# Receptance units on halves of the array's rows, spread between score chunks, in an attention and channel-mix kernel

## Chip, core and metric

The kernel runs on one core of one Trainium2 chip. The metric is the device time of one execution in microseconds, the median of several runs.

## What is computed

Sigmoid attention over 8 batches, 12 heads, 448 positions and 64 columns per head, and then an RWKV-like channel mix on its output x (8 x 448 x 768). Weights come as 64-bit floats.

```python
scores = q @ k.T / sqrt(64) - log(448)
x = sigmoid(scores) @ v                 # heads side by side: 768 columns
x_prev = x shifted by one position in each batch
xk = mu_k * x + (1 - mu_k) * x_prev
xr = mu_r * x + (1 - mu_r) * x_prev
kk = maximum(xk @ w_k, 0)               # 768 -> 1024
v = kk * kk @ w_v                       # 1024 -> 768
r = sigmoid(xr @ w_r)                   # 768 -> 768, the receptance
out = r * v
```

## The kernel before

Heads are taken in pairs: "head n" in the code and here is a pair of heads laid on the two halves of the 128 partitions, 48 of them, six to a batch. Positions 0 to 383 of the keys are three chunks of 128 (NC = 3), the last 64 are the tails.

`prepare` (L304) splits k and q of a head into a high part of type fp32r (ScalarE cast, L308) and the rest, the low part (VectorE subtraction, L309). `scores` (L332) multiplies one chunk of keys with all queries: three products (high-high, low-high, high-low), each as two matmuls, one for each half of the rows (64 partitions), into the two banks of a score tile `sc[u]`. `sigmoid` (L349) reads both banks with one ScalarE instruction of 896 columns into a tile `pf`. `weigh` (L362) multiplies a chunk of `pf` with v, the two heads on the two halves of the array's columns. The tails of two heads go through `score_tails` and `weigh_tails` on quarters of the array. `gather` (L379) takes the attention output of a head out of the bank, stores it to memory, forms xr and splits that too; for heads under R_FROM = 10 most of it is on ScalarE, from there on more is on VectorE.

There are three tiles `sc`, of two banks each. `turn` (L328) hands them out round: each user waits until the one three turns before it has been read.

A receptance unit (`receptance`, L398) is one block of 128 output columns of r for one batch: six blocks of xr, three matmuls for each (L406 to L408), on all 128 rows, 18 in all, into one bank; a sigmoid on ScalarE (L412) and a store of r follow. There are 48 units. 40 are placed in the attention, two in each loop from n=8 on; the last eight follow it, in a plan of their own.

The main loop (L470) takes two heads at a time, n = 0, 2, ..., 46. In it TensorE's order is: three chunks of scores of head n+1; then two receptance units (n >= 8) or the weighing of head n (n < 8); three chunks of scores of head n+2; weighings that are left; tails of the weighing (L374); tail scores of heads n+2 and n+3 (`last_keys`, L345). A light loop is here one without a receptance unit, a heavy loop one with.

Every step is handed to `Plan` with an engine, an estimated cost, a priority (about the number of the head at which it is due, small first) and what it reads and writes. `Plan.order` simulates the engines with these costs and writes out a fixed order for each engine; all engines then run their list in order. TensorE's steps depend on each other in a chain, so its order is that of the program text. SWITCH (L209) is an estimate of 190 ns that the plan adds to a step at which the use of the array's rows and columns changes.

`convert_wr` (L248) turns w_r from 64-bit floats into fp32r parts (five VectorE steps, a ScalarE cast, a VectorE subtraction), twelve pieces, with due times WR_PACE apart. `convert_seven` (L259) does the same for w_k and w_v, and stores sums that the second half needs; its due times begin after R_FROM (L447). After the attention the channel mix runs with seven products per block (L633), in a plan that has nothing of the change.

Of the kernel before, what the change touches and what calls it, by code (L numbers as in the profile page):

```python
# [10 lines left out]
AF = mybir.ActivationFunctionType  # L11
# [11 lines left out]
class Plan:  # L23
# [8 lines left out]
    def op(self, engine, cost, prio, run, reads, writes, dma=None):  # L32
        i = len(self.ops)
        deps = set()
        for r in reads:
            if r in self.writer:
                deps.add(self.writer[r])
        for w in writes:
            if w in self.writer:
                deps.add(self.writer[w])  # L40
            deps.update(self.readers.get(w, ()))
        for r in reads:
            self.readers.setdefault(r, []).append(i)
        for w in writes:
            self.writer[w] = i
            self.readers[w] = []
        deps.discard(i)
        self.ops.append(Op(engine, cost, prio, run, deps, dma))
# [50 lines left out]
def attention_then_channel_mix(  # L99
# [14 lines left out]
    nc = tc.nc  # L114
    P = 128
    N, _, S = q.shape
# [6 lines left out]
    NJ = DM // P  # L123
    NF = DF // P
    NC = S // P
# [25 lines left out]


    WP, PFB, PTB, LEAD, RAW = 512, 9, 2, 2, 4
    WR_PACE, W_PACE = 0.85, 0.9
    R_FROM = 10
    LATE = 2


# [52 lines left out]
    def mm(n, cols=S):  # L211
        return n * (cols * 0.447 + 3)

    def act(n, sbuf=False, ptr=False):
        return 51 + 0.834 * n + 42 * sbuf + 93 * ptr

    def dve(n, fast=False, ptr=False):
        return 69 + n / (1.92 if fast else 0.96) + 61 * ptr

    def dma(dst, src, prio, reads, writes):  # L220
        ns = dst.shape[0] * math.prod(dst.shape[1:]) * 4 / 300
        op(SP, 500, prio, lambda: nc.sync.dma_start(dst, src), reads, writes, dma=ns)
# [81 lines left out]
    def prepare(n, at):  # L304
        i = n % LEAD
        for src, hi, lo, a, w in ((kn[n % RAW][:, :KW], kh, kl, "k", KW), (qn[n % RAW], qh, ql, "q", S)):
            R = [(a + "n", n % RAW)]
            op(ACT, act(w, True), at, lambda src=src, hi=hi: nc.scalar.copy(hi[i], src), R, [(a + "h", i)])  # L308
            op(DVE, dve(w), at, lambda src=src, hi=hi, lo=lo: nc.vector.tensor_sub(lo[i], src, hi[i]), R + [(a + "h", i)], [(a + "l", i)])  # L309

    half = [slice(h * D, (h + 1) * D) for h in range(2)]
# [1 line left out]
    def pe(cost, go, reads, writes, at):  # L313

        op(PE, cost, at, go, reads, writes + ["order"])
# [5 lines left out]
    def qk(n):  # L321
        i = n % LEAD
        return [(a, i) for a in ("kh", "kl", "qh", "ql")]
# [4 lines left out]
    def turn():  # L328
        turns[0] += 1
        return (turns[0] - 1) % 3  # L330

    def scores(n, c, u, at):  # L332
        def go():
            for e, (kk, qq) in enumerate(products(n)):
                for h in range(2):
                    nc.tensor.matmul(sc[u][:, h, :S], kk[half[h], c * P:(c + 1) * P], qq[half[h], :], start=e == 0, stop=e == 2)  # L336

        pe(mm(3) + SWITCH * (c == 0), go, qk(n), [("sc", u, 0), ("sc", u, 1)], at)


    def score_tails(n, u, at):
# [7 lines left out]
    def sigmoid(n, c, u, at):  # L349
        if c < NC:  # L350
            i = (n * NC + c) % PFB
            f, K = pf[i], ("pf", i)
        else:
            i = n // 2 % PTB
            f, K = pt[i], ("pt", i)
        R = [("sc", u, 0), ("sc", u, 1)]
        op(ACT, act(2 * S), at, lambda: nc.scalar.activation(f, sc[u][:, :, :S], AF.Sigmoid, bias=NEG_LOG_S, scale=SCALE), R, [K])  # L357


    def weigh(n, c, at):  # L360
        i = (n * NC + c) % PFB

        def go():
            for h in range(2):
                nc.tensor.matmul(av[n % 2][half[h], :S], vn[n % 5][:, h * NC + c, :], pf[i][:, h, :], start=c == 0, stop=False)  # L365

        pe(752 + SWITCH * (c == 0) * (n % 2 == 0 or n < 8), go, [("pf", i), ("vn", n % 5)], [("av", n % 2)], at)


    def weigh_tails(n, at):  # L370
# [8 lines left out]
    def gather(n, at):  # L379
        b, j = divmod(n, NP)  # L380
        x, y = xx[n % 2], t1[n % 2]
        X, T = ("xx", n % 2), ("t1", n % 2)
        if n < R_FROM:
            op(ACT, act(S), at, lambda: nc.scalar.copy(x[:, 1:], av[n % 2][:, :S]), [("av", n % 2)], [X])  # L384
        else:
            op(DVE, dve(S), at, lambda: nc.vector.tensor_copy(x[:, 1:], av[n % 2][:, :S]), [("av", n % 2)], [X])  # L386
        dma(x_d[j][b], x[:, 1:], at, [X], [("x_d", n)])
        if n < R_FROM:
            op(ACT, act(S, True, True), at, lambda: nc.scalar.mul(y, x[:, :S], omr[:, j:j + 1]), [X, ("om", 0)], [T])  # L389
        else:  # L390
            op(DVE, dve(S, True, True), at, lambda: nc.vector.tensor_scalar(y, x[:, :S], omr[:, j:j + 1], None, ALU.mult), [X, ("om", 0)], [T])
        op(DVE, dve(S, ptr=True), at, lambda: nc.vector.scalar_tensor_tensor(y, x[:, 1:], mur[:, j:j + 1], y, ALU.mult, ALU.add), [X, T], [T])
        t, key = xr[j][:, :, b % 2 * S:(b % 2 + 1) * S], ("xr", j, b % 2)
        op(ACT, act(S, True), at, lambda: nc.scalar.copy(t[:, 0], y), [T], [key + ("hi",)])
        op(DVE, dve(S), at, lambda: nc.vector.tensor_sub(t[:, 1], y, t[:, 0]), [T, key + ("hi",)], [key + ("lo",)])

    def receptance(b, i, at, bank):
        t, tk = bank  # L398
# [44 lines left out]
    for nh in range(2):  # L443
        for j in range(NJ):
            convert_wr(j, nh, jt)
            jt += WR_PACE
    jt = max(R_FROM, jt)  # L447
    for w, out7, half_rows, n in ((w_k, wk_o, NJH, DF // 2), (w_v, wv_o, NFH, HN)):
        for t in range(half_rows):
            convert_seven(w, out7, t, half_rows, n, W_PACE, jt + 0.4)  # L450
# [1 line left out]
    units = [(b, i) for b in range(B - 1) for i in range(NJ)]  # L452
    late = units[len(units) - LATE:]
    units = units[:len(units) - LATE]
    def key_chunks(n, at):
        if n + 1 < N:
            prepare(n + 1, at + 0.6 - 5 * (n < R_FROM))
        us = [turn() for _ in range(NC)]
        for c in range(NC):
            scores(n, c, us[c], at)  # L460
            sigmoid(n, c, us[c], at + 0.1 * c)

    def last_keys(n, at):
        u = turn()
# [3 lines left out]
    key_chunks(0, 0)  # L468
    last_keys(0, 0)
    for n in range(0, N, 2):  # L470
        at = n + 1
        key_chunks(n + 1, at)
        if n + 3 < N:
            load(n + 3, at + 0.2 - 5 * (n < 4))
        if n >= 8:
            for _ in range(2):
                u = turn()
                if units:
                    receptance(*units.pop(0), at + 0.4, (sc[u][:, 0], ("sc", u, 0)))
        else:  # L480
            for c in range(NC):
                weigh(n, c, at)
        at = n + 2
        if n + 2 < N:
            key_chunks(n + 2, at)
        for i in range(n < 8, 2):
            for c in range(NC):
                weigh(n + i, c, at)
        weigh_tails(n, at)
        if n + 2 < N:  # L490
            last_keys(n + 2, at)
        if n + 4 < N:
            load(n + 4, at + 0.2 - 5 * (n < 4))
        gather(n, at + 0.45)
        gather(n + 1, at + 0.5)
# [246 lines left out]
```

## Time and profile before

| | |
|---|---|
| median of 3 runs | 854.35 us (852.76 to 854.6) |
| the profiled execution | 852.26 us |
| its span, first to last instruction | 850.5 us |
| TensorE busy | 834.7 us (98%) |
| VectorE busy | 600.5 us (71%) |
| ScalarE busy | 447.6 us (53%) |
| granted TensorE clock | 1.0 of full |
| attention, with its receptance units | about 0 to 412 us |
| last units and passage to the channel mix | about 412 to 450 us |
| channel mix | about 450 to 850 us |

A busy TensorE is one with a matmul in it; matmuls overlap, so a start-to-start time says what one costs, and its listed duration does not. ScalarE and VectorE instructions overlap their neighbours a little as well. An idle time in a row stands in square brackets behind it, with what ended it. PEld is the loading of weights into the array.

### The profile page before, as it was taken

How to read it: one execution, taken by the hardware profiler on the slowest of the kernel's cores; microseconds unless marked ns; L12 is line 12 of the kernel's file. 1: busy time of each engine (PE TensorE's matmuls, PEld its weight loads, DVE VectorE, ACT ScalarE, POOL GpSimd, SP SyncE). 2: the span in 40 equal slices, each digit the busy share in tenths (PEclk: the TensorE clock that was granted, in tenths of full speed). 3: DMA queues.
4: the chain of work that ended last, by engine and by line, in shares of the span. 5: the costliest groups of instructions: out<-in, count | busy, mean ns of one | idle time of the engine just before them, and what ended most of it. 6: DMA issues, size and time to landing. Idle time of an engine off the chain costs nothing.

```text
span 850.5 us, 13233 instructions
## 1 busy us (share of the span) xinstructions
PE 834.7 (98%) x4704; PEld 667.2 (78%) x4704; DVE 600.5 (71%) x1115; ACT 447.6 (53%) x758; POOL 0.5 (0%) x8
## 2 busy tenths in 40 slices
PE   7999999999999999999999999999999999999998
PEld 3456666776667776677789999999999999999997
DVE  5999888988334333342379987969789795886955
ACT  7995555655546555464378394563746333333330
POOL 0000000000000000000000000000000000000000
PEclk9999999999999999999999999999999999999999
DMA  8878898888334433341487553343654667473415
GB/s 256 257 242 285 295 310 281 285 288 281 122 111 154 151 118 118 109 141 44 153 286 246 166 183 101 138 140 120 217 181 147 204 184 239 135 238 121 141 60 163
DMA packets 90930, 157.65 MB, mean 185 GB/s; under 512 B 10352, under 2 KB 79472, under 8 KB 90864
## 3 DMA queue, kind: packets, MB, share of 16 engines
q1 hardware_dynamic: 90864, 156.81, 56.4%
q8 instruction: 37, 0.61, 0.3%
q14 instruction: 29, 0.24, 0.1%
HBM read 98.05 MB, written 58.72 MB: 184 GB/s over the span
## 4 chain that ended last, share of the span: by engine, by line
PE 90%; ACT 4%; DMA 3%; issue 1%; DVE 1%; SPq 0%; POOLq 0%; POOL 0%; DVEq 0%; ACTq 0%
PE xb L633 26%; PE yb L633 20%; PE av L365 12%; PE sc L336 10%; PE sc L406 6%; PE sc L407 6%; PE sc L408 6%; DMA x<-x_d 2%; PE av L374 2%; PE sc L345 2%; ACT pf L357 1%; ACT t L389 1%; DMA qn<-in_q 1%; ACT qh L308 0%; ACT xx L384 0%
## 5 line engine op out<-in xcount | busy, mean ns | idle before, releaser
L557 ACT CAST rr<-ys 128x448 fp32r<-128x448 f32 x135 | 73.8, 567 | 106.7 <-PE xb L633 41.6
L357 ACT ACTIVATE pf<-sc 128x896 f32<-128x896 f32 x144 | 125.5, 926 | 5.1 <-PE sc L336 5.1
L365 PE MATMUL av<-pf,vn 128*64 128x448 f32 x576 | 114.4, 544 | 0.0
L406 PE MATMUL sc<-xr,slot 128*128 128x448 f32 x288 | 106.6, 370 | 2.1 <-ACT pf L357 2.1
L407 PE MATMUL sc<-xr,slot 128*128 128x448 f32 x288 | 104.3, 362 | 0.0
L408 PE MATMUL sc<-xr,slot 128*128 128x448 f32 x288 | 104.2, 362 | 0.0
L633 PE MATMUL xb<-rr,slotc 128*128 128x448 f32 x450 | 93.0, 362 | 0.4 <-ACT p1s L662 0.4
L633 PE MATMUL yb<-rr,slot 128*128 128x448 f32 x450 | 92.9, 362 | 0.0
L558 DVE TENSOR_TENSOR rr<-ys,rr 128x448 fp32r<-128x448 f32 x135 | 80.4, 618 | 16.0 <-ACT rr L557 15.9
L309 DVE TENSOR_TENSOR kl<-kn,kh 128x384 fp32r<-128x384 f32 x48 | 26.7, 556 | 88.9 <-ACT kh L308 88.8
L633 PEld LDWEIGHTS xb<-rr,slotc 128*128 128x128 f32 x450 | 84.3, 187 | 6.4 <-ACT p1s L662 0.8
L633 PEld LDWEIGHTS yb<-rr,slot 128*128 128x128 f32 x450 | 84.4, 187 | 5.6
L365 PEld LDWEIGHTS av<-pf,vn 128*64 128x64 f32 x576 | 38.9, 136 | 62.4 <-issue 61.3
L336 PE MATMUL sc<-qh,kh 64*128 64x448 f32 x288 | 59.3, 408 | 7.0 <-ACT qh L308 4.5
L412 ACT ACTIVATE ro<-sc 128x448 f32<-128x448 f32 x48 | 26.1, 545 | 74.1 <-PE sc L408 61.7
L406 PEld LDWEIGHTS sc<-xr,slot 128*128 128x128 f32 x288 | 54.0, 188 | 12.6 <-ACT pf L357 8.3
L357 ACT ACTIVATE pt<-sc 128x896 f32<-128x896 f32 x24 | 22.2, 925 | 75.4 <-PE sc L345 75.4
L386 DVE COPY xx<-av 128x448 f32<-128x448 f32 x38 | 22.0, 621 | 50.4 <-PE av L374 50.4
L408 PEld LDWEIGHTS sc<-xr,slot 128*128 128x128 f32 x288 | 54.0, 187 | 3.7
L336 PEld LDWEIGHTS sc<-qh,kh 64*128 64x128 f32 x288 | 27.3, 186 | 37.5 <-issue 19.1
L407 PEld LDWEIGHTS sc<-xr,slot 128*128 128x128 f32 x288 | 54.1, 188 | 3.1
L336 PE MATMUL sc<-ql,kh 64*128 64x448 f32 x288 | 53.3, 366 | 0.0
(86 smaller groups left out, 1374.6 us busy)
## 6 DMA issues: line engine op xcount, KB each, us to landing
k_d<-cc SPq DMA_DIRECT2D x64, 224.0 KB, 2.0
kn<-in_k SPq DMA_DIRECT2D x48, 224.0 KB, 4.5
qn<-in_q SPq DMA_DIRECT2D x48, 224.0 KB, 4.7
vn<-in_v SPq DMA_DIRECT2D x48, 224.0 KB, 3.4
x_d<-xx SPq DMA_DIRECT2D x48, 224.0 KB, 3.8
r_d<-ro SPq DMA_DIRECT2D x48, 224.0 KB, 2.7
x<-x_d SPq DMA_DIRECT2D x48, 224.0 KB, 2.7
rt<-r_d SPq DMA_DIRECT2D x48, 224.0 KB, 2.9
```

The lines of the kernel that those rows point to most:

```text
L309: op(DVE, dve(w), at, lambda src=src, hi=hi, lo=lo: nc.vector.tensor_sub(lo[i], src, hi[i]), R + [(a + "h", i)], [(a + "l", i)])
L336: nc.tensor.matmul(sc[u][:, h, :S], kk[half[h], c * P:(c + 1) * P], qq[half[h], :], start=e == 0, stop=e == 2)
L357: op(ACT, act(2 * S), at, lambda: nc.scalar.activation(f, sc[u][:, :, :S], AF.Sigmoid, bias=NEG_LOG_S, scale=SCALE), R, [K])
L365: nc.tensor.matmul(av[n % 2][half[h], :S], vn[n % 5][:, h * NC + c, :], pf[i][:, h, :], start=c == 0, stop=False)
L386: op(DVE, dve(S), at, lambda: nc.vector.tensor_copy(x[:, 1:], av[n % 2][:, :S]), [("av", n % 2)], [X])
L406: nc.tensor.matmul(t[:, :S], wr_hi[j][:, rows], hi, start=(j == 0), stop=False)
L407: nc.tensor.matmul(t[:, :S], wr_lo[j][:, rows], hi, start=False, stop=False)
L408: nc.tensor.matmul(t[:, :S], wr_hi[j][:, rows], lo, start=False, stop=(j == NJ - 1))
L412: op(ACT, act(S), at, lambda: nc.scalar.activation(ro[u], t[:, :S], AF.Sigmoid), [tk], [("ro", u)])
L557: op(ACT, act(S, True), at, lambda: nc.scalar.copy(r[:, 0], y), [Y], [R])
L558: op(DVE, dve(S), at, lambda: nc.vector.tensor_sub(r[:, 1], y, r[:, 0]), [Y, R], [R + ("lo",)])
L633: nc.tensor.matmul(bank[:, :S], a, b, start=first and t == 0 and e == 0, stop=t == n - 1 and e == 2, skip_group_check=True)
```

## The change

It has four parts.

- A unit becomes `receptance_halves`: every matmul of it is cut into two, one for each half of the 128 rows, as the scores are. The halves' sums go into the two banks of one tile `sc[u]`. ScalarE copies one bank to `ro`, VectorE adds the other, ScalarE takes the sigmoid in place. The eight units after the attention keep the old form.
- Units stand apart from each other: in a heavy loop one after the third score chunk of head n+1 and one after the first score chunk of head n+2.
- Loops with units begin at n=10 instead of n=8; loops 10 and 12 have three units (the third after the second chunk of head n+2). Loop 8 weighs head n between the score chunks, as loops 0 to 6 do. The 40 units stay 40.
- For heads 2 to 8 the casts of q and k run on VectorE. Due times of the weight conversions move (WR_PACE 0.9, begin of w_k and w_v after R_FROM + 1), and the plan's SWITCH estimates follow the new order.

```diff
-    WR_PACE, W_PACE = 0.85, 0.9
+    WR_PACE, W_PACE = 0.9, 0.9
     R_FROM = 10
+    CAST_DVE = "qk"
...
+    def copy_on(e, dst, src):
+        (nc.scalar.copy if e == ACT else nc.vector.tensor_copy)(dst, src)
+
+    def copy_cost(e, n):
+        return act(n, True) if e == ACT else dve(n, True)
...
-            op(ACT, act(w, True), at, lambda src=src, hi=hi: nc.scalar.copy(hi[i], src), R, [(a + "h", i)])
+            e = DVE if a in CAST_DVE and 2 <= n < R_FROM - 1 else ACT
+            op(e, copy_cost(e, w), at, lambda e=e, src=src, hi=hi: copy_on(e, hi[i], src), R, [(a + "h", i)])
...
-        pe(mm(3) + SWITCH * (c == 0), go, qk(n), [("sc", u, 0), ("sc", u, 1)], at)
+        pe(mm(3) + SWITCH * (c == 0) * (n % 2 == 1 or n < R_FROM), go, qk(n), [("sc", u, 0), ("sc", u, 1)], at)
...
+    def receptance_halves(b, i, at, u):
+        t, tk = sc[u], [("sc", u, 0), ("sc", u, 1)]
+        o = (b * NJ + i) % 2
+        rows, x = slice(i * P, (i + 1) * P), slice(b % 2 * S, (b % 2 + 1) * S)
+        for j in range(NJ):
+            keys = [("xr", j, b % 2, a) for a in ("hi", "lo")]
+
+            def go(j=j):
+                for e, (w, a) in enumerate(((wr_hi, 0), (wr_lo, 0), (wr_hi, 1))):
+                    for h in range(2):
+                        nc.tensor.matmul(t[:, h, :S], w[j][half[h], rows], xr[j][half[h], a, x], start=(j, e) == (0, 0), stop=(j, e) == (NJ - 1, 2))
+
+            nh = i * P // HN
+            pe(mm(3), go, keys + [("wr", j, nh), (("wr", j, nh), "lo")], tk, at)
+        op(ACT, act(S), at, lambda: nc.scalar.copy(ro[o], t[:, 1, :S]), tk, [("ro", o)])
+        op(DVE, dve(S), at, lambda: nc.vector.tensor_add(ro[o], t[:, 0, :S], ro[o]), tk + [("ro", o)], [("ro", o)])
+        op(ACT, act(S, True), at, lambda: nc.scalar.activation(ro[o], ro[o], AF.Sigmoid), [("ro", o)], [("ro", o)])
+        dma(r_d[i][b], ro[o], at, [("ro", o)], [("r_d", i, b)])
...
-    jt = max(R_FROM, jt)
+    jt = max(R_FROM + 1, jt + 1)
...
-    def key_chunks(n, at):
+    def key_chunks(n, at, between=()):
+
         if n + 1 < N:
             prepare(n + 1, at + 0.6 - 5 * (n < R_FROM))
-        us = [turn() for _ in range(NC)]
         for c in range(NC):
-            scores(n, c, us[c], at)
-            sigmoid(n, c, us[c], at + 0.1 * c)
+            u = turn()
+            scores(n, c, u, at)
+            sigmoid(n, c, u, at + 0.1 * c)
+            if c in between and units:
+                receptance_halves(*units.pop(0), at + 0.1 * c, turn())
...
-        at = n + 1
-        key_chunks(n + 1, at)
+        at, R = n + 1, n >= R_FROM
+        key_chunks(n + 1, at, (NC - 1,) if R else ())
...
-        if n >= 8:
-            for _ in range(2):
-                u = turn()
-                if units:
-                    receptance(*units.pop(0), at + 0.4, (sc[u][:, 0], ("sc", u, 0)))
-        else:
+        if not R:
             for c in range(NC):
                 weigh(n, c, at)
         at = n + 2
         if n + 2 < N:
-            key_chunks(n + 2, at)
-        for i in range(n < 8, 2):
+            key_chunks(n + 2, at, ((0, 1) if n < R_FROM + 4 else (0,)) if R else ())
+        elif units:
+            receptance_halves(*units.pop(0), at, turn())
+        for i in range(n < R_FROM, 2):
             for c in range(NC):
                 weigh(n + i, c, at)
```

## Rows read from the trace of the kernel before

**Rows 1.** Windows of 25 us: length; busy PE, PEld, DVE, ACT, POOL (instructions); clock; DMA.

```profile
25.00:50.00 25.00, 22.89 (x158) 10.22 (x154) 24.52 (x53) 24.74 (x44) 0.00 (x0) 1.00 0.78 250
...
150.00:175.00 25.00, 25.00 (x150) 18.68 (x148) 23.17 (x51) 13.39 (x22) 0.00 (x0) 1.00 0.90 293
...
300.00:325.00 25.00, 25.00 (x164) 15.29 (x164) 7.60 (x15) 13.19 (x21) 0.00 (x0) 1.00 0.31 103
```

**Rows 2.** Timeline of TensorE: start, duration; tail scores, at the end of loops.

```profile
20.53 0.93 PE L345 MATMUL sc<-qn,kn 64*64 64x448 f32 x8
...
55.94 0.93 PE L345 MATMUL sc<-qn,kn 64*64 64x448 f32 x8
...
74.84 0.93 PE L345 MATMUL sc<-qn,kn 64*64 64x448 f32 x8
...
93.75 0.93 PE L345 MATMUL sc<-qn,kn 64*64 64x448 f32 x8
...
111.52 0.93 PE L345 MATMUL sc<-qn,kn 64*64 64x448 f32 x8
```

**Rows 3.** Timeline of one repeating loop, first score chunk to the second head's scores.

```profile
290.20 0.92 ACT L357 ACTIVATE pt<-sc 128x896 f32<-128x896 f32 x1 [4.19 <-PE sc L345]
...
291.02 1.72 ACT L357 ACTIVATE pf<-sc 128x896 f32<-128x896 f32 x2
...
291.56 0.36 PE L336 MATMUL sc<-qh,kl 64*128 64x448 f32 x2
...
291.76 0.36 PE L336 MATMUL sc<-ql,kh 64*128 64x448 f32 x2
...
292.05 0.47 PE L406 MATMUL sc<-xr,slot 128*128 128x448 f32 x1
...
292.36 0.36 PE L407 MATMUL sc<-xr,slot 128*128 128x448 f32 x1
...
299.16 0.37 PE L408 MATMUL sc<-xr,slot 128*128 128x448 f32 x1
...
299.46 0.47 PE L336 MATMUL sc<-qh,kh 64*128 64x448 f32 x2
```

**Rows 4.** Timelines of a light loop: ScalarE's score sigmoids, TensorE's second three chunks.

```profile
37.45 2.55 ACT L357 ACTIVATE pf<-sc 128x896 f32<-128x896 f32 x3
...
38.43 0.47 PE L336 MATMUL sc<-qh,kh 64*128 64x448 f32 x2 [0.78 <-ACT pf L357]
...
39.24 0.47 PE L336 MATMUL sc<-qh,kh 64*128 64x448 f32 x2
39.55 0.36 PE L336 MATMUL sc<-qh,kl 64*128 64x448 f32 x2
```

**Rows 5.** Timeline of TensorE: the first unit of loop 10.

```profile
78.86 0.47 PE L406 MATMUL sc<-xr,slot 128*128 128x448 f32 x1 [1.04 <-ACT pf L357]
```

**Rows 6.** Timeline of ScalarE in a light loop, between first and second score sigmoid.

```profile
23.37 0.94 ACT L357 ACTIVATE pf<-sc 128x896 f32<-128x896 f32 x1
24.17 0.53 ACT L308 CAST kh<-kn 128x384 fp32r<-128x384 f32 x1
24.58 0.59 ACT L308 CAST qh<-qn 128x448 fp32r<-128x448 f32 x1
25.04 0.54 ACT L255 CAST slot<-wbits 128x384 fp32r<-128x384 f32 x1
25.45 0.59 ACT L394 CAST xr<-t 128x448 fp32r<-128x448 f32 x1
25.92 0.69 ACT L389 ACTIVATE t<-xx,omr 128x448 f32<-128x448 f32 x1
26.49 1.74 ACT L357 ACTIVATE pf<-sc 128x896 f32<-128x896 f32 x2
```

**Rows 7.** Groups of instructions by line and shape: two VectorE steps of the gather.

```profile
L386 DVE COPY xx<-av 128x448 f32<-128x448 f32 x38 | 22.0, 621 | 50.4 <-PE av L374 50.4
...
L391 DVE TENSOR_SCALAR t<-xx,omr 128x448 f32<-128x448 f32 x38 | 15.3, 445 | 0.0
```

More of the change, by code (lines that the diff above doesn't have):

```diff
@@ L365, in go @@
                 nc.tensor.matmul(av[n % 2][half[h], :S], vn[n % 5][:, h * NC + c, :], pf[i][:, h, :], start=c == 0, stop=False)
-        pe(752 + SWITCH * (c == 0) * (n % 2 == 0 or n < 8), go, [("pf", i), ("vn", n % 5)], [("av", n % 2)], at)
+        pe(752 + SWITCH * (c == 0) * (n % 2 == 0 or n < R_FROM), go, [("pf", i), ("vn", n % 5)], [("av", n % 2)], at)
     def weigh_tails(n, at):
```

## The prediction

> **What bounds the kernel now.** I read the windows first [rows 1]. TensorE is busy for all of the 25 us at 150 and at 300, at the full granted clock, and so from about 100 us to the end of the attention; only the opening shows holes (22.89 of 25 us), and there ScalarE (24.74) and VectorE (24.52) are both full. VectorE stays above 90% while the weights are converted (23.17 of 25 in the window at 150 us) and falls to 7.60 at 300 us. So there are two regimes: an opening set by ScalarE, and a long stretch in which the time is the sum of what TensorE issues. In the second, only fewer or cheaper TensorE steps move the end.
>
> Next I took the length of each loop over a pair of heads from the starts of the tail scores at its end [rows 2]. Loops n=2, 4 and 6 take 55.94-20.53 = 35.41 us, 11.8 each, loop 8 18.90, loop 10 18.91, loop 12 17.77. Loops 14 to 44 repeat loop 12. Loops up to 6 hold no receptance unit, loops from 8 on two each.
>
> Then one repeating loop in order of time [rows 3]. Pairs of score matmuls, each on 64 rows, start every 0.20 us (291.56, 291.76); so do single receptance matmuls on 128 rows (292.36 to 299.16, 34 steps: 0.200). At the border from scores to receptance the step is 0.29 instead of 0.20 and the next one 0.31; from receptance back to scores 0.30 (299.16 to 299.46), and the step after it is as long. A border costs about 0.20 us.
>
> **The change, TensorE part.** A unit keeps 18 steps: 18 full matmuls become 18 pairs of half-row matmuls. By the score pairs a pair costs 0.20 us, as a full matmul does, so 40 units x 18 steps cost nothing more. That is the price I take; the other end is that the halves do not run together, 0.40 per pair, 720 x 0.20 = 144 us. The score rows have the same shape (64 rows, 128 weight columns, 448 columns, a bank for each half), so I stay at the first, with one reserve: those runs are 9 pairs long and the new ones 45.
>
> The Trainium skill's TensorE: Matmul & The Clock Gate, section LDWEIGHTS, speaks against the change: a load takes as long as its columns need, about 107 ns for 128, however few rows it fills. If the two loads of a pair followed each other, a pair would be estimated at 213 ns, 13 ns over the full matmul, and 720 pairs would add some 9 us. The score rows, two loads each at 0.20, show no sign of that.
>
> Borders: receptance and scores now use the array in the same way, so scores-receptance and receptance-scores are no longer changes. By count a loop loses two, 0.41 us. But only one of them is free of another wait. The first unit of a loop uses the bank pair of the first score chunk, three turns back. That pair is read by a sigmoid which follows the sigmoid of the tails: 290.20, then 291.02 plus 0.92 = 291.94, and in a stalled case TensorE starts 0.06 after ScalarE ends (37.45 plus 0.92 is 38.37, the chunk starts at 38.43 [rows 4]). So the unit could not start before 292.00; it does start at 292.05 [rows 3]. Where TensorE waits in an unchanged mode, the step after the stall is 0.31 as well (39.24 to 39.55 [rows 4]). So the first border keeps all but 0.05 us: the wait takes its place. The second saves 0.22 (0.10 + 0.11, rounded up). I take 0.27 per loop; ends 0.20 and 0.43. Seventeen loops (12 to 44): 4.6 us, ends 3.4 and 7.3. Loop 46 changes from two units to two units with the first border only: 0.05, left out.
>
> Evacuation: one sigmoid becomes a ScalarE copy, a VectorE add and a sigmoid. The two ScalarE instructions are at most 0.93 us each by the 896-column sigmoid [rows 6], the add about 0.62 by the VectorE copy out of PSUM [rows 7]; the chain is under 2.5 us. Who waits: the chunk that takes the unit's bank pair three turns later, which is 0.6 + 3.6 = 4.2 us after the unit's end, since another unit lies between. So it is hidden, with 1.7 us to spare, and outside that cover costs what exceeds it. Behind the sigmoid that waits for the add stand score sigmoids on ScalarE; in loops from 10 on ScalarE is half idle (13.19 of 25 [rows 1]), and the next urgent pair (tails, first chunk) comes about 7 us later: the loop less its receptance and its score pairs, 17.77-7.2-3.6, lies between. The store of r moves about 1.5 us later in SP's queue; the loads behind it are for heads two or more ahead. I cost this at nothing.
>
> **The change, opening.** For heads 2 to 8 the two casts of q and k go from ScalarE to VectorE. On ScalarE they occupy 24.17 to 25.04, 0.87 us per head [rows 6], and stand between the first and second score sigmoid; TensorE's second half of the loop waits for that second sigmoid (idle 0.78 us in [rows 4], and then 0.81 per chunk, from 38.43 to 39.24, which is ScalarE's pace, instead of 3 x 0.20). Casts run about two heads ahead, so the heads 2 to 8 are cast in loops 0, 2 and 4, and heads 9 to 12 in loops 6 and 8, still on ScalarE. Without stalls a light loop is a heavy one without its 7.2 us of receptance, 17.77-7.2 = 10.6 us less some rounding in its borders, 10.5. ScalarE's own sum, from start to start in [rows 6], is seven sigmoids at 0.80, four casts of 0.41 or 0.46, three weight casts of 0.41, and for two gathered heads two copies (taken as 0.41), two products of 0.57 and two casts of 0.47: 11.5 us, about the 11.8 of the loop. Without the four casts, and with one weight cast less, it is 9.3. TensorE becomes the later of the two, with a rest of stall, since the gather's cast and product stay in front of the second sigmoid. I take 10.6 for loops 2 and 4 (-2.3), 0.8 for loop 0, 0.4 for loop 6 with one weight cast less: 3.5 us. Ends: 1.0 (the loops only lose part of a stall) and 4.7 (all four at 10.5).
>
> VectorE is as full there. What it gains per head is two casts: between 0.62 each (the copy out of PSUM) and 0.30 (the single-source instruction of 448 columns, 0.445 with a per-partition scalar and overlap [rows 7]). I take 0.35, nearest to the latter, as it too reads and writes SBUF. The Trainium skill's VectorE: DVE Perf Modes, section on the perf-mode tier table, gives an fp32 copy within SBUF double rate; whether a cast to fp32r counts is not stated, and no row shows it. Seven heads: 4.9 us, ends 4.2 and 8.7. They displace weight conversions, which the plan puts in wherever VectorE is free. Of the twelve of w_r, six are needed by the first unit in loop 10, and all by loop 12; at two per loop instead of three they are in time. Those of w_k and w_v are over before 300 us (7.60 of VectorE there [rows 1]), and the channel mix that needs them begins after 410. So nothing on the path, as long as VectorE's order leaves lows and gathers in time.
>
> **Units moved.** Loop 8 loses its two units, loops 10 and 12 get three. Loops 8 and 10 were 37.81 us. Loop 8 is now light with the casts still on ScalarE, 11.4; loop 10 is 18.91 + 3.60 - 0.2 = 22.3, as its first unit still finds ScalarE busy with the gather of heads 8 and 9 (the 1.04 us stall [rows 5] stays, the one in loop 8 goes); loop 12 adds 3.6. Together 37.3: 0.5 us, ends -0.5 and 1.4. The later pacing of conversions changes due times of work with slack: nothing.
>
> **Sum.** 4.6 + 3.5 + 0.5 = 8.6 us; ends 3.9 and 13.4. The channel mix after it is not touched and starts when the attention ends. The profiled execution took 852.26 us (span 850.5 and 1.8 around it), so 843.7 against that one; it lies 2.1 under the median of the runs, 854.35, from which I forecast 845.7.
>
> **Rivals.** (1) The first border is free too, and the opening runs at TensorE's sum: 13.4 us, 841.0. For it: a reordered ScalarE queue could bring the first sigmoid earlier. Against it: the chain tails, sigmoid, sigmoid [rows 3] is not shortened by the change. 0.17.
> (2) VectorE becomes the bound of the opening: of the 8.7 us that 14 casts at 0.62 take, conversions with slack give way to most; if a quarter stays on the path, the opening gains nothing and loses about 2 us, and the repeating loops still give 4.6: 851.8. For it: 24.52 of 25 [rows 1]. Against: conversions have slack. 0.10.
> (3) The border is not a matter of how the array is divided, but of changing operands and banks. Then the repeating loops keep 17.77, and only opening and moved units count: 850.4. Against: chunk to chunk, which changes banks and weights, costs nothing where no wait is due. 0.08.
> (4) Slower: long runs of half-row pairs do not hold 0.20. A loop now issues 45 pairs, 180 loads and matmuls, behind a wait, where the trace shows no more than 36 in a run. Each 10 ns per pair costs 7.2 us over 720 pairs; from 12 ns on the gain is gone, and at 20 ns the time is 860.2. Against: three pairs directly after a stall keep 0.20 to 0.21. The Trainium skill's rule on loads, named above, would be one such cause. 0.10.
>
> **How the numbers follow.** The forecast has 0.55, the rivals 0.17, 0.10, 0.08, 0.10. A difference under 0.2% (1.7 us) is about what a measurement of this kernel can tell from none. Faster by more: 0.55 + 0.17 + most of (3) + two fifths of (2) = 0.82; within: 0.06; slower: rival (4) and a rest of (2), 0.12. The range goes from 839.5 (rival 1, with 1.5 for the spread of the runs) to 853.0 (rivals 2 and 3 in it), leaving out (4).
>
> **What would show it.** Right: no longer step at a receptance-score border in loops from 14 on, a loop of 17.5, the first unit of a loop still ended by ScalarE's first score sigmoid; light loops near 10.6 with no 0.8 stall; casts near 0.35 on VectorE. Wrong: pairs above 0.20 inside a unit (4), loops of 17.34 (1), of 17.77 (3), TensorE waiting for the lows of q or k in the opening (2), or ScalarE waiting for the add while TensorE stands.

## The result, and the profile after

The changed kernel takes 844.78 us (median of 4 runs, 844.2 to 845.61) against 854.32 us (4 runs): ratio 0.990, interval 0.9885 to 0.9914. The forecast was 845.7 us. The profiled execution took 845.33 us with a span of 843.6, 6.9 under the span before; the medians of this comparison lie 9.5 apart, and those of a second comparison (e5 below) 7.2. The forecast gain of 8.6 lies among the three.

The page of the changed kernel, engine totals and the row of the new unit's weight loads (busy us, mean ns of one | idle before them):

```profile
PE 829.8 (98%) x5424; PEld 668.5 (79%) x5424; DVE 626.3 (74%) x1169; ACT 462.1 (55%) x784; POOL 0.5 (0%) x8
...
L416 PEld LDWEIGHTS sc<-xr,slot 64*128 64x128 f32 x1440 | 133.3, 184 | 14.5 <-ACT pf L365 5.4
```

There are 720 matmuls more (5424 against 4704), and TensorE's busy time is 829.8 us; the loads of the new unit are listed at 184 ns each.

Windows of 25 us, columns as in [rows 1], which they answer to:

```profile
25.00:50.00 25.00, 24.71 (x176) 12.05 (x176) 24.28 (x57) 22.80 (x38) 0.00 (x0) 1.00 0.83 283
...
150.00:175.00 25.00, 25.00 (x216) 17.82 (x214) 23.89 (x51) 15.87 (x27) 0.00 (x0) 1.00 0.84 281
...
300.00:325.00 25.00, 25.00 (x222) 17.84 (x222) 12.84 (x24) 15.77 (x25) 0.00 (x0) 1.00 0.49 158
```

TensorE's hole in the opening is down from 2.1 us to 0.3, ScalarE has come down from 24.74 to 22.80, VectorE is as full as before. After 225 us VectorE has room.

One repeating loop in order of time (answers to [rows 3]; x36 is one unit, its 18 pairs):

```profile
285.21 1.72 ACT L365 ACTIVATE pf<-sc 128x896 f32<-128x896 f32 x2
...
285.97 0.37 PE L344 MATMUL sc<-ql,kh 64*128 64x448 f32 x2
...
286.18 3.89 PE L416 MATMUL sc<-xr,slot 64*128 64x448 f32 x36
...
289.70 0.19 PEld L344 LDWEIGHTS sc<-qh,kh 64*128 64x128 f32 x2
...
289.91 0.36 PE L344 MATMUL sc<-qh,kh 64*128 64x448 f32 x2
...
290.15 0.53 ACT L420 COPY ro<-sc 128x448 f32<-128x448 f32 x1 [0.62 <-ACT qh L222]
...
290.50 3.77 PE L416 MATMUL sc<-xr,slot 64*128 64x448 f32 x36
...
290.72 0.62 DVE L421 TENSOR_TENSOR ro<-sc,ro 128x448 f32<-128x448 f32 x1 [0.53 <-ACT ro L420]
...
294.11 0.37 PE L344 MATMUL sc<-qh,kh 64*128 64x448 f32 x2
```

From the first unit to the next score chunk there are 3.73 us, of which 18 pairs at 0.20 make 3.60; from the second unit's start to the next chunk 3.61, nothing but its pairs. The border from unit to scores is gone: the weights of the first score pair are loaded at 289.70, 0.21 before its matmul. The first unit starts 0.21 after the pair before it. A rest of 0.12 us remains there against the second unit, in the step after its start (0.31 instead of 0.20), and the sigmoid of the first chunk ends at 285.21 + 0.92 = 286.13, 0.05 before the unit starts. The unit's banks are copied from 290.15 and added by 291.34, 2.8 us before the chunk that takes them (294.11).

Second halves of the light loops 2 and 6 (score chunks' first pairs on TensorE; they answer to [rows 4]):

```profile
25.28 0.47 PE L344 MATMUL sc<-qh,kh 64*128 64x448 f32 x2
...
25.99 0.36 PE L344 MATMUL sc<-qh,kh 64*128 64x448 f32 x2
...
26.59 0.36 PE L344 MATMUL sc<-qh,kh 64*128 64x448 f32 x2
...
47.89 0.47 PE L344 MATMUL sc<-qh,kh 64*128 64x448 f32 x2 [0.28 <-ACT pf L365]
```

In loop 2 the chunks follow at 0.71 and 0.60 us without a wait. In loop 6, whose casts are still on ScalarE, a wait of 0.28 is left. The casts themselves, grouped by engine and shape:

```profile
L222 ACT CAST qh<-qn 128x448 fp32r<-128x448 f32 x41 | 23.9, 583 | 0.7 <-DMA qn<-in_q 0.6
...
L222 ACT CAST kh<-kn 128x384 fp32r<-128x384 f32 x41 | 21.3, 520 | 2.4 <-DMA kn<-in_k 2.4
...
L222 DVE CAST qh<-qn 128x448 fp32r<-128x448 f32 x7 | 2.7, 390 | 0.0
L222 DVE CAST kh<-kn 128x384 fp32r<-128x384 f32 x7 | 2.5, 363 | 3.0 <-PE sc L344 3.0
```

Loop lengths from the starts of the tail scores, for all kernels that were run (us; the last column is where the last tail scores start):

| kernel | first start | 0 | 2 | 4 | 6 | 8 | 10 | 12 | 14 to 44, typical | last start |
|---|---|---|---|---|---|---|---|---|---|---|
| before | 8.79 | 11.74 | 11.76 | 11.78 | 11.87 | 18.90 | 18.91 | 17.77 | 17.77 | 395.76 |
| changed | 8.49 | 11.51 | 10.50 | 10.95 | 11.26 | 11.74 | 22.85 | 21.14 | 17.49 | 388.27 |
| e1 casts only | 8.37 | 11.13 | 10.51 | 11.63 | 11.26 | 18.72 | 18.85 | 17.77 | 17.77 | 392.48 |
| e2 no casts | 9.40 | 12.67 | 11.78 | 11.77 | 11.86 | 10.99 | 22.14 | 21.09 | 17.49 | 391.52 |
| e3 halves adjacent | 8.87 | 12.61 | 11.78 | 11.77 | 11.87 | 19.74 | 19.05 | 18.32 | 17.89 to 18.48 | 401.66 |
| e4 units from 8 | 8.76 | 10.86 | 10.50 | 11.76 | 11.27 | 18.47 | 18.64 | 17.48 | 17.49 | 387.61 |
| e5 changed again | 8.80 | 10.87 | 10.50 | 11.19 | 11.26 | 11.73 | 22.90 | 21.09 | 17.49 | 388.09 |
| e6 full units, spread | 8.92 | 12.57 | 10.50 | 11.44 | 11.26 | 11.74 | 23.61 | 22.21 | 18.18 | 403.13 |
| e7 short tail sigmoid | 9.16 | 10.66 | 10.50 | 10.81 | 10.90 | 11.36 | 22.33 | 21.05 | 17.44 | 385.88 |
| e8 unit earlier | 8.29 | 10.86 | 10.50 | 10.75 | 11.28 | 11.73 | 23.36 | 21.35 | 17.75 | 392.32 |
| e9 from 8, gather | 8.76 | 10.86 | 10.50 | 11.11 | 11.34 | 18.03 | 17.47 | 17.49 | 17.49 | 385.30 |
| e10 gather of 8, 9 | 9.06 | 12.74 | 10.50 | 11.13 | 11.27 | 11.73 | 26.56 | 21.09 | 17.49 | 393.85 |

### The profile page after: what moved, and what is told of

The parts are those of the page before. It is cut to its first block, busy times and chain, and to the rows that moved or that the text cites. A ratio compares the mean times of both kernels' runs of the same rounds, so it can differ in the third digit from the quotient of the medians.

```text
span 843.6 us, 14697 instructions
## 1 busy us (share of the span) xinstructions
PE 829.8 (98%) x5424; PEld 668.5 (79%) x5424; DVE 626.3 (74%) x1169; ACT 462.1 (55%) x784; POOL 0.5 (0%) x8
## 4 chain that ended last, share of the span: by engine, by line
PE 88%; DVE 5%; DMA 4%; ACT 2%; issue 1%; SPq 0%; POOLq 0%; DVEq 0%; POOL 0%; ACTq 0%
PE xb L661 26%; PE yb L661 20%; PE sc L416 17%; PE av L373 11%; PE sc L344 9%; DMA x<-x_d 2%; PE av L382 2%; PE sc L353 2%; DMA wraw<-in_moe_w_r 1%; DVE wbits L243 1%; DVE wbits L244 0%; DVE xr L403 0%; DVE wbits L245 0%; ACT pf L365 0%; DVE ql L317 0%
## 5 line engine op out<-in xcount | busy, mean ns | idle before, releaser
L416 PE MATMUL sc<-xr,slot 64*128 64x448 f32 x1440 | 152.7, 362 | 1.0 <-ACT pf L365 1.0
L416 PEld LDWEIGHTS sc<-xr,slot 64*128 64x128 f32 x1440 | 133.3, 184 | 14.5 <-ACT pf L365 5.4
L365 ACT ACTIVATE pf<-sc 128x896 f32<-128x896 f32 x144 | 128.2, 924 | 3.0 <-PE sc L344 1.9
L344 PE MATMUL sc<-qh,kh 64*128 64x448 f32 x288 | 57.3, 394 | 5.8 <-ACT qh L222 4.8
L365 ACT ACTIVATE pt<-sc 128x896 f32<-128x896 f32 x24 | 22.1, 922 | 70.6 <-PE sc L353 70.6
L421 DVE TENSOR_TENSOR ro<-sc,ro 128x448 f32<-128x448 f32 x40 | 24.9, 623 | 47.4 <-ACT ro L420 47.2
L420 ACT COPY ro<-sc 128x448 f32<-128x448 f32 x40 | 21.4, 535 | 57.9 <-issue 35.4
L344 PE MATMUL sc<-qh,kl 64*128 64x448 f32 x288 | 53.0, 365 | 0.0
L661 PE MATMUL xb<-rr,slotb 128*128 128x448 f32 x225 | 46.5, 362 | 2.1 <-issue 2.1
L661 PEld LDWEIGHTS xb<-rr,slotb 128*128 128x128 f32 x225 | 42.1, 187 | 5.2 <-issue 2.4
```

Of the source, the lines that this page charges most:

```text
L416: nc.tensor.matmul(t[:, h, :S], w[j][half[h], rows], xr[j][half[h], a, x], start=(j, e) == (0, 0), stop=(j, e) == (NJ - 1, 2))
L420: op(ACT, act(S), at, lambda: nc.scalar.copy(ro[o], t[:, 1, :S]), tk, [("ro", o)])
L421: op(DVE, dve(S), at, lambda: nc.vector.tensor_add(ro[o], t[:, 0, :S], ro[o]), tk + [("ro", o)], [("ro", o)])
L661: nc.tensor.matmul(bank[:, :S], a, b, start=first and t == 0 and e == 0, stop=t == n - 1 and e == 2, skip_group_check=True)
```

## The experiments

**e1 and e2: the casts, and everything but the casts.** e1 is the kernel before with the lines of `copy_on`, `copy_cost` and `prepare`; e2 is the changed kernel with

```diff
-    CAST_DVE = "qk"
+    CAST_DVE = ""
```

> The kernel before with one part of the change alone: the casts of q and k of heads 2 to 8 on VectorE. Theory (the opening is set by ScalarE, VectorE has only conversions with slack to give up): loops 0, 2, 4 and 6 take about 11.5, 10.5, 10.9 and 11.3 us as in the changed kernel, loops 12 to 44 stay at 17.77, so about 3.2 us less than before, ratio 0.996. Rival (VectorE is as full as ScalarE there, so the casts only move the wait; the changed kernel's light loops are short for another reason): loops 2 to 6 stay near 11.8, ratio 1.000 or above.

> The changed kernel with all casts back on ScalarE. Theory: loops 2 to 6 back at 11.8 us and loop 8 with them, loops 14 to 44 at 17.49; 0.28 x 17 = 4.7 us less than before, less some 0.5 lost by the units moved, so 4.2, ratio 0.995. Rival (the casts matter for the heavy loops too, as the order of ScalarE and VectorE hangs together): loops 14 to 44 not at 17.49.

e1: 850.51 us, ratio 0.9968 (0.9958 to 0.9979). e2: 847.68 us, ratio 0.9939 (0.9927 to 0.9951). e1 keeps 17.77 in the heavy loops and e2 keeps 11.8 in loops 2 to 6, as expected. Two loops came out otherwise: loop 4 of e1 takes 11.63 instead of 10.9, loop 8 of e2 10.99 instead of 11.8. In the traces the last tail scores start 3.28 us earlier in e1 and 4.24 in e2, together 7.52, and 7.49 in the changed kernel. That this fits so well is chance, for e2 lost 1.5 us before loop 2 for a reason that is not the casts (last section). Counted from the start of loop 2, e1 gains 2.25 us, e2 5.78, and both together 6.95. So the two halves do touch each other, in loops 8 and 10: they take 11.74 and 22.85 us in the changed kernel and 10.99 and 22.14 in e2, although the casts put on VectorE are those of earlier loops.

**e3: halves, but units next to each other.** The kernel before with `receptance_halves` called where it called `receptance`:

```diff
-                    receptance(*units.pop(0), at + 0.4, (sc[u][:, 0], ("sc", u, 0)))
+                    receptance_halves(*units.pop(0), at + 0.4, u)
```

> The kernel before with units on halves of the rows, but still two next to each other from loop 8 on, after the third score chunk of head n+1. Theory: the border from unit to scores costs nothing, as in the changed kernel (0.22 less), the first border keeps ScalarE's wait (0.05 less), but the third score chunk of head n+2 now takes the second unit's banks 1.2 us after the unit ends, and copy, add and their hand-overs take about 1.3: a stall of some 0.1 with the 0.11 step after it. Loops of 17.6 to 17.75 us, ratio 0.997 to 1.000. Rival (keeping units apart does nothing): 17.49 as in the changed kernel, ratio 0.994. Other rival (the borders are not due to the division of the array): 17.77 and more.

857.9 us, ratio 1.0054 (1.004 to 1.0068): slower than before. The timeline after the second unit of a loop:

```profile
286.60 0.36 PE L336 MATMUL sc<-qh,kh 64*128 64x448 f32 x2
...
286.85 0.53 ACT L411 COPY ro<-sc 128x448 f32<-128x448 f32 x1 [1.81 <-PE sc L407]
...
287.41 0.62 DVE L412 TENSOR_TENSOR ro<-sc,ro 128x448 f32<-128x448 f32 x1 [2.98 <-ACT ro L411]
287.60 0.36 PE L336 MATMUL sc<-ql,kh 64*128 64x448 f32 x2
...
288.09 0.47 PE L336 MATMUL sc<-qh,kh 64*128 64x448 f32 x2
...
288.40 0.37 PE L336 MATMUL sc<-qh,kl 64*128 64x448 f32 x2
```

The third chunk should start at 287.80 and starts at 288.09. ScalarE's copy begins 0.25 us after TensorE has gone on, VectorE's add ends at 288.03, TensorE starts 0.06 later: 1.49 us from the end of the unit, where the two chunks between cover 1.2. The stall is 0.29, and the step after it 0.31, so 0.40 in all: 17.49 + 0.40 = 17.89, the loop measured once VectorE has room. While it converts weights the add stands behind other work, and loops take up to 18.48. I expected 17.6 to 17.75 and a ratio of 1.000 at most, since I had put the chain at 1.3 and not counted the wait for VectorE.

**e4 and e5: units from loop 8 on; the changed kernel again.** e4:

```diff
-        at, R = n + 1, n >= R_FROM
+        at, R = n + 1, n >= 8
...
-            key_chunks(n + 2, at, ((0, 1) if n < R_FROM + 4 else (0,)) if R else ())
+            key_chunks(n + 2, at, (0,) if R else ())
```

> The changed kernel with two units in each loop from n=8 on, instead of none in loop 8 and three in loops 10 and 12. Theory: moving units was not what gained; loops 8 and 10 take 17.5 and the 1.0 us that the first unit waits for ScalarE, loop 12 17.5, together 54.6 against 55.7 in the changed kernel: 1.0 us less than the changed kernel, ratio to before 0.988. Rival (the weights of the receptance are late when VectorE makes the casts, so units in loop 8 wait for them): loop 8 over 20 us, ratio 0.992 or above.

> The changed kernel itself, beside the three that follow on one chip. Loops 14 to 44 at 17.49 us; ratio to before 0.989 to 0.991.

e4: 845.82 us, ratio 0.9919 (0.9906 to 0.9931), where 0.988 was expected. e5: 845.7 us, 0.9913 (0.9896 to 0.9929). Loops 8 to 12 take 54.59 us in e4 (54.6 expected) against 55.73 in the changed kernel, but they begin 0.4 to 0.5 us later, and the last tail scores start only 0.5 to 0.7 us earlier; the ratio doesn't tell the two apart. Moving units neither gained nor cost what can be measured. In loop 8 the first unit waits 0.85 us for a score sigmoid, not for its weights.

**e6: spread, but full matmuls.**

```diff
-                receptance_halves(*units.pop(0), at + 0.1 * c, turn())
+                v = turn()
+                receptance(*units.pop(0), at + 0.1 * c, (sc[v][:, 0], ("sc", v, 0)))
```

> The changed kernel with every unit in its place but in the old form (full matmuls on 128 rows, one bank, one sigmoid). Theory (a border between a use of all rows and a use of halves costs 0.2 us, whatever stands on both sides): a repeating loop has two borders more than the kernel before, four in all at the units; loops 14 to 44 take 17.77 + 0.4 = 18.17 us, loops 10 and 12 0.2 to 0.4 more than that for their third unit, so about 0.7 x 17 = 11.6 us more than the changed kernel, ratio to before 1.004. Rival (the border comes from operands or banks, and spreading or evacuation removed it): loops stay near 17.5.

859.95 us, ratio 1.008 (1.006 to 1.0101), above the 1.004 expected; the loop takes 18.18 us, as expected. Of what the attention is longer than in the changed kernel, the sixteen loops make 11.0 us, loops 10 and 12 1.8, and the part before loop 2, which has no unit, 1.5 (last section). The border from the second unit to the scores, where nothing is waited for:

```profile
305.06 0.37 PE L436 MATMUL sc<-xr,slot 128*128 128x448 f32 x1
305.35 0.19 PEld L344 LDWEIGHTS sc<-qh,kh 64*128 64x128 f32 x2 [0.30 <-issue]
305.35 0.47 PE L344 MATMUL sc<-qh,kh 64*128 64x448 f32 x2
...
305.66 0.36 PE L344 MATMUL sc<-qh,kl 64*128 64x448 f32 x2
```

0.29 and 0.31 again instead of 0.20. The weights of the first pair are not loaded ahead here: load and matmul both start at 305.35, while in the changed kernel the load at this place came 0.21 before its matmul. Two borders more than before, 17.77 + 0.41: with the same tensors the border comes and goes with the division of the array. A unit here also has one bank where it has two in the changed kernel, but chunk follows chunk at 0.20 with a change of banks. The four borders make 0.69 over the changed kernel, in which the wait stands at the first of them.

**e7: the tails' sigmoid halved** (the last 224 of the 448 columns of each bank are left out and stay at zero, so this kernel leaves out part of the attention).

```diff
-        op(ACT, act(2 * S), at, lambda: nc.scalar.activation(f, sc[u][:, :, :S], AF.Sigmoid, bias=NEG_LOG_S, scale=SCALE), R, [K])
+        w = S if c < NC else S // 2
+        op(ACT, act(2 * S), at, lambda: nc.scalar.activation(f[:, :, :w], sc[u][:, :, :w], AF.Sigmoid, bias=NEG_LOG_S, scale=SCALE), R, [K])
```

> The changed kernel in which ScalarE's sigmoid of the tail scores takes half of the columns; the other half stays zero, so part of the attention of the tails is left out. Theory (the first unit of a loop waits for the sigmoid of the tails and then that of the first score chunk): the second sigmoid ends about 0.37 us earlier, the unit starts 0.20 after the last score pair, and the step after it is 0.20: loops 14 to 44 take 17.34 to 17.36 us, 0.14 less than in the changed kernel; 2.3 us in all. Rival (the 0.31 step there is a border of TensorE's own or a matter of issue): 17.49 unchanged.

844.01 us, ratio 0.9895 (0.9878 to 0.9912), loops of 17.44, not 17.34 to 17.36. The entry of the first unit:

```profile
282.25 0.55 ACT L368 ACTIVATE pt<-sc 128x448 f32<-128x448 f32 x1 [3.92 <-PE sc L355]
...
282.60 0.36 PE L346 MATMUL sc<-ql,kh 64*128 64x448 f32 x2
...
283.00 1.73 ACT L368 ACTIVATE pf<-sc 128x896 f32<-128x896 f32 x2 [0.21 <-PE sc L346]
...
283.80 0.37 PE L346 MATMUL sc<-ql,kh 64*128 64x448 f32 x2
283.98 3.51 PEld L419 LDWEIGHTS sc<-xr,slot 64*128 64x128 f32 x36 [0.19 <-ACT pf L368]
284.00 3.86 PE L419 MATMUL sc<-xr,slot 64*128 64x448 f32 x36
...
287.70 0.36 PE L346 MATMUL sc<-qh,kh 64*128 64x448 f32 x2
```

The unit now starts 0.20 after the last score pair, but it still takes 3.70 us to the next chunk. The tails' sigmoid is out of the way by 282.80, and yet the next begins at 283.00: it waits for its own chunk, whose last pair starts at 282.60, and ends at 283.92. So there are two waits nearly on top of each other. Without the sigmoid of the tails, a chunk's own hand-over (0.40), its sigmoid (0.92) and the way back (0.06) take 1.38 from its last pair, about the 1.40 to the unit's turn. The weights are loaded only when the wait is over (283.98, with the matmul at 284.00), and 0.10 stays.

**e8: the first unit one chunk earlier, the banks freed by two copies.**

```diff
-        key_chunks(n + 1, at, (NC - 1,) if R else ())
+        key_chunks(n + 1, at, (1,) if R else ())
...
-        op(DVE, dve(S), at, lambda: nc.vector.tensor_add(ro[o], t[:, 0, :S], ro[o]), tk + [("ro", o)], [("ro", o)])
+        op(DVE, dve(S), at, lambda: nc.vector.tensor_copy(rs[0], t[:, 0, :S]), tk, [("rs", 0)])
+        op(DVE, dve(S), at, lambda: nc.vector.tensor_add(ro[o], rs[0], ro[o]), [("rs", 0), ("ro", o)], [("ro", o)])
...
-    wbits = ring(cpool, "wbits", 8, [P, WP], U32)
+    wbits = ring(cpool, "wbits", 7, [P, WP], U32)
```

> The changed kernel with the first unit of a loop one chunk earlier (after the second score chunk of head n+1), where its banks are those of the tails, already read; the second unit then takes the first one's banks 1.2 us after it ends, so copy and add are replaced by two copies side by side, one on ScalarE and one on VectorE, and an add afterwards (one buffer of converted weights less, for room). Theory: no wait of the unit for ScalarE; the two copies free the banks in about 0.9 us, where the chain of copy and add took 1.49 when measured with adjacent units; loops from 24 on, with VectorE not full, take 17.34 us, loops 14 to 22 between 17.34 and 17.7 as VectorE's queue delays its copy; about 1 to 2 us less than the changed kernel. Rival (first border is TensorE's own): 17.49 at best.

850.14 us, ratio 0.9968 (0.9954 to 0.9983), loops of 17.75. First and second unit of a loop:

```profile
287.79 0.37 PE L345 MATMUL sc<-ql,kh 64*128 64x448 f32 x2
287.81 3.58 PEld L417 LDWEIGHTS sc<-xr,slot 64*128 64x128 f32 x36
...
288.00 3.77 PE L417 MATMUL sc<-xr,slot 64*128 64x448 f32 x36
...
291.61 0.37 PE L345 MATMUL sc<-qh,kh 64*128 64x448 f32 x2
...
291.86 0.53 ACT L421 COPY ro<-sc 128x448 f32<-128x448 f32 x1 [1.56 <-issue]
...
292.42 0.62 DVE L422 COPY rs<-sc 128x448 f32<-128x448 f32 x1 [1.40 <-ACT ro L421]
...
292.62 0.37 PE L345 MATMUL sc<-ql,kh 64*128 64x448 f32 x2
...
293.10 3.88 PE L417 MATMUL sc<-xr,slot 64*128 64x448 f32 x36
```

The first half came as expected: no wait, the weights are loaded 0.19 before the matmul (287.81, 288.00), the unit starts 0.21 after the last score pair and takes 3.61 us to the next chunk. That border is wholly gone. The second half failed: VectorE's copy starts 0.03 after ScalarE's ends, though it needs nothing of it, so the banks are free at 293.04 and the second unit starts 0.48 instead of 0.20 after the last chunk, with 0.31 behind it. 17.34 + 0.40 = 17.74, about the 17.75 measured. It is the program that puts the two copies one behind the other: in the trace VectorE's copy waits for one semaphore, the one that ScalarE's instructions count up, and for none of TensorE's, while ScalarE's copy waits for TensorE. Both read the same tile. Whether the chip would run them side by side was not tried.

**e9 and e10: the stall before the first unit of loops 8 and 10.** Both take the gather of early heads to VectorE, e9 on top of e4 for heads 6 to 9, e10 in the changed kernel for heads 8 and 9 (8 in place of 6 in the edit):

```diff
-        if n < R_FROM:
+        if n < 6:
```

> Units from loop 8 on, two per loop, and the gather of heads 6 to 9 as it is for later heads (copy and product on VectorE). Theory (the stall of the first unit in loops 8 and 10 is the gather's work in front of the first score sigmoid on ScalarE, as in the rows of the kernel before): loops 8 and 10 take 17.5 to 17.8 us where units from 8 on alone gave 18.47 and 18.64; ratio to before about 0.990, 1.5 to 2 us less than the changed kernel. Rival (VectorE, full with conversions, then does the gather late and the stall comes back as a wait for it): loops 8 and 10 at 18.4 or more, ratio 0.992.

> The changed kernel with the gather of heads 8 and 9 on VectorE. Theory: the first unit of loop 10 no longer waits 1.0 us for ScalarE; loop 10 takes 21.8 to 22.2 us where the changed kernel took 22.85, the rest as there; ratio to before about 0.990. Rival: loop 10 stays at 22.9.

e9: 842.8 us, ratio 0.9888 (0.9871 to 0.9905), the shortest of all, with loops 8 and 10 at 18.03 and 17.47 (17.5 to 17.8 expected; in loop 8 a score chunk waits 0.27 us for the add of a unit); the last tail scores start 2.3 us before those of e4. e10: 848.86 us, ratio 0.9954 (0.9942 to 0.9967); loop 10 takes 26.56, where 21.8 to 22.2 was expected. The first unit's wait for ScalarE is gone, but another wait has come. TensorE there, and VectorE's two low parts:

```profile
71.66 0.70 PE L344 MATMUL sc<-ql,kh 64*128 64x448 f32 x2 [3.69 <-DVE ql L317]
72.16 0.58 PE L344 MATMUL sc<-qh,kh 64*128 64x448 f32 x2
72.53 0.58 PE L344 MATMUL sc<-qh,kl 64*128 64x448 f32 x2
...
66.73 0.55 DVE L317 TENSOR_TENSOR kl<-kn,kh 128x384 fp32r<-128x384 f32 x1
...
70.99 0.62 DVE L317 TENSOR_TENSOR ql<-qn,qh 128x448 fp32r<-128x448 f32 x1
```

TensorE waits 3.69 us for the low part of q, and on VectorE eight instructions, conversions and gather, stand between the low part of k and that of q. The order is fixed ahead, with VectorE full; the same move that helped in e9 put a step that TensorE needs behind work that nothing waited for.

## Why the prediction was right, point by point

**Repeating loops: right.** 17.50 forecast, 17.49 measured; 0.28 in each of 16 loops and 0.23 in loop 12 (21.14 less a unit of 3.60), 4.7 us against 4.6. In the rows the second border gave 0.21 (0.22 forecast) and the first 0.08 (0.05). That the first border stays because of ScalarE was argued from 0.05 us between two rows. e8, where the first unit stands one chunk earlier and has nothing to wait for, shows it; e7 shows that I had only half of the wait.

**A pair costs what a full matmul costs: right.** 18 pairs in 3.61 us, in runs of 45. Rival (4), the slower side, falls: the two loads of a pair are listed at 0.184 us each (page of the profile, above) and start 0.003 us apart, and pairs still start every 0.20. The Trainium skill's rule for a load's time (TensorE: Matmul & The Clock Gate, section LDWEIGHTS, about 107 ns for 128 columns) does not give the listed time, and the sum of two loads does not set the step of a pair here.

**Evacuation at nothing: right, for the reason given.** In the loop shown the banks are free 1.43 us after TensorE has gone on (289.91 to 291.34), and in e3 the whole way from unit to next user takes 1.49; the chunk and the unit between cover 4.2. The 2.5 of the prediction counted the last sigmoid too, which no longer holds the banks. The cover is not safe with any order: in e9, with the gather on VectorE, one chunk of loop 8 waits 0.27 for the add. e3 is the price without the cover: 0.40 per loop and up to 1.0 while VectorE is full, 10.2 us in all against e2 (857.9 less 847.68), which has its casts on ScalarE too; enough to turn the gain into a loss. e3 and e2 differ in more than this (loops 8 to 12, due times), but the wait for the add is in e3's rows. Putting the units apart, which by itself costs 0.41 per loop (e6), is what lets the halves pay.

**Opening: right in kind, 3.5 forecast, 3.2 measured.** Loops 2 and 4 give 2.1 (2.3 forecast), loop 6 0.6 (0.4); e5 and e1 give 2.5 and 2.0 for the three. For loop 0 0.8 was forecast; the first tail scores start 0.30 earlier and loop 0 gives 0.23, but these 0.5 cannot be told from the spread: the second tail scores start at 19.2 to 22.1 us in the twelve traces, and the four late ones (21.5 to 22.1: e2, e3, e6, e10) have the casts on either engine (last section). Casts take 0.39 and 0.36 us on VectorE against 0.58 and 0.52 on ScalarE, so the 0.35 taken, near the cheap end of my bounds, was about right. The Trainium skill's VectorE: DVE Perf Modes, section on the perf-mode tier table, gives an fp32 copy within SBUF double rate; the rows agree for a cast to fp32r, at 0.39 us where VectorE's subtraction over the same 448 columns (ql) takes 0.62. Rival (2) falls: the opening gains.

**Moved units, and conversions at nothing: wrong sign, small.** Forecast 0.5 gained; loops 8 and 10 and the added unit of loop 12 take 11.74 + 22.85 + 3.60 = 38.19 against 37.81, so 0.4 lost. Loop 8 was put at 11.4 and took 11.74; loop 10 was put at 22.3 and took 22.85. Its entry:

```profile
66.28 0.47 PE L344 MATMUL sc<-ql,kh 64*128 64x448 f32 x2 [0.30 <-DVE ql L317]
...
68.96 1.27 PE L416 MATMUL sc<-xr,slot 64*128 64x448 f32 x10 [1.00 <-ACT pf L365]
```

The stall of 1.00 is the one I had counted; the 0.30 for the low part of q is the wait that I named as a sign of rival (2) and priced at nothing. e10 shows how large that can become. But the moving itself was not at fault: in e2, with all casts on ScalarE, the same loops take 10.99 + 22.14 + 3.60 = 36.73, 1.1 us less than before, and the first unit waits 0.33 instead of 1.00. The 1.5 us between e2 and the changed kernel come with the casts on VectorE. They put off conversions of weights, whose casts are ScalarE's: in loop 8 ScalarE makes three of these (two in e2) and waits of TensorE for score sigmoids appear (0.28 and 0.39), and in loop 10 it makes one, and six casts of q and k (none and four in e2). So, as far as these rows show, the term that failed is the displaced conversions, "nothing on the path" in the prediction: they cost about 1.5 us.

**After the attention: "starts when the attention ends" was only nearly so.** The attention is shorter by 7.5 us, the span by 6.9. The last unit and the first product of the channel mix:

```profile
432.75 0.37 PE L436 MATMUL sc<-xr,slot 128*128 128x448 f32 x1
435.20 7.45 PE L661 MATMUL xb<-rr,slotb 128*128 128x448 f32 x36 [2.08 <-issue]
```

TensorE idles 2.08 us there, 1.44 in the kernel before. The steps before that product begin with a load of x, for which ScalarE waits 3.05 us in the changed kernel and 2.43 before; why the load lands later was not tried. e5, the same kernel, idles 2.06, so this 0.6 need not be chance. From the last tail scores to the end the twelve traces have between 454.0 us (e2) and 456.3 (e1), with no order among them that follows the edits, and the two traces of the changed kernel have 455.3 and 456.1. The medians spread too (the kernel before has 854.32 us beside the changed kernel and 852.87 beside e5), so 7.2 and 9.5 can both stand for one change.

**Rival (3)** falls with e6, **rival (1)** with 17.49 against 17.34. Against the profiled execution, which is what the sum was made for, the sum was 1.7 too large: 0.3 in the opening, 0.9 in the moved units, 0.6 in the passage, less 0.1 in the loops (8.6 against 6.9 of span). That the median came within 1 us of the forecast is in part luck, by the spread of the medians.

## What to carry to other kernels

A change of how the array is divided costs a step of its own, so work that can be cut to the same division should stand next to work that has it; but count only those borders at which nothing else is waiting. Before cutting a matmul into halves whose sum has to be made afterwards, measure the time from its last matmul to the release of its banks and see that the steps until their next use are longer; the order of the steps decides whether the cut pays. An engine that is full with work that can wait may be given more, as long as the steps that TensorE needs soon stand in front in its order; then look where the work that gave way turns up again, for it may be on another engine (here ScalarE, in loops 8 and 10).

## What the runs showed of the hardware that was not expected

A wait just long enough to be met in time is not free: a matmul whose weights were not loaded ahead (e7, load and matmul 0.02 us apart) is followed by a step of 0.28, one whose weights were loaded 0.19 ahead (e8) by 0.20. The border in e6 looks the same in this respect (load and matmul at 305.35, the next step 0.31), though nothing is waited for. That the late load is the cause of the longer step is read from these rows; no run changes the load alone.

After the stall of 3.69 us in e10 TensorE's pairs start every 0.37 us instead of 0.20. Windows after it (length, PE, PEld, DVE, ACT, POOL, clock, DMA share, GB/s):

```profile
71.60:74.00 2.40, 2.34 (x12) 2.13 (x14) 2.40 (x7) 1.60 (x3) 0.00 (x0) 0.53 0.98 352
...
78.00:82.00 4.00, 4.00 (x44) 3.99 (x42) 3.23 (x7) 1.92 (x3) 0.00 (x0) 1.00 0.46 158
```

From 67 to 71.6 us TensorE was busy for 0.97 of 4.6 us, with the clock at 1.00. Then the granted clock is 0.53 of full, the lower of its two levels (1.2 GHz of 2.4) for most of the stretch, 0.71 from 74 to 76 us and full from 76 us on. In the changed kernel it is 1.00 in the same windows. So loop 10 of e10 lost not only the 3.69 us of its wait.

The same step of 0.37 us opens all twelve traces: the first score pairs, from about 4.5 to 8 us, start that far apart. In e2, e3, e6 and e10 the pairs of loop 0 still do, here in e2:

```profile
11.74 0.58 PE L344 MATMUL sc<-qh,kl 64*128 64x448 f32 x2
12.12 0.58 PE L344 MATMUL sc<-ql,kh 64*128 64x448 f32 x2
```

In the other eight they start about every 0.20 there. The clock column shows 1.00 in both cases, so the records do not say why, and the four share no edit that the others lack. It puts the start of loop 2 1 to 3 us later, where the whole opening gained 3.2.
